# Full-array attention-output products, a four-accumulator first output block and a split last output in a fused attention and feed-forward kernel

## The chip, the cores and the metric

The kernel runs on one core of a Trainium2 chip. The time is the device time of an execution in microseconds; a profile counts from the start of its span, which is about 2 us shorter than the device time. Each kernel ran several times, and runs over 1.5% above the fastest run of the same kernel are left out of comparisons. An eviction is the copy of a result out of PSUM, which frees its buffer. Engines: PE is TensorE (PEld its weight loads), DVE VectorE, ACT ScalarE, POOL GpSimd, SP the engine that issues most transfers.

## The reference

Attention with both softmaxes taken separately (over the head dimension for q, over the sequence for k), so that each head needs only a 64x64 matrix `kv`; then a feed-forward block over all 4,608 tokens. The code is condensed.

```python
batch, n_heads, seq, head_dim = (8, 8, 576, 64)
kv = np.einsum('bhsd,bhse->bhde', k_s, v)          # k_s: softmax over seq
attn = np.einsum('bhsd,bhde->bhse', q_s, kv)       # q_s: softmax over d
x = attn.transpose(0, 2, 1, 3).reshape(B * S, H * D)
h = x @ w_in                                       # 512 -> 2048
g = h + sin(alpha * h) ** 2 / (alpha + 1e-09)
out = g @ w_out                                    # 2048 -> 512
```

## The kernel before

Tokens go in nine tiles of 512. In a tile, "hp" products (h, transposed) go through ACT (sine), one of ACT, POOL or DVE (square) and DVE (combine, which writes g and frees the PSUM buffer of hp). "op" products multiply the g of the previous tile with w_out. The attention of a later batch is woven in: kvp products, kv_norm, then four calls of attn_out per batch, whose result xp is copied to xT, the input of hp. The code below is cut, and its comments are added.

```python
    def attn_out(b, ii, half, pool, eng):
        ...
        xp = pool.tile([128, 2, 512], F32, name="xp", tag="a")
        for x in range(2):
            r = slice(64 * x, 64 * x + 64)
            for e in range(2):
                nc.tensor.matmul(xp[64 * e:64 * e + 64, x, 0:n], kt[r, e, ii, :],
                                 qT[r, j0:j1, ii, e * 64:(e + 1) * 64], start=True, stop=True)
        eng(xT[:, ii::2, c0:c0 + n], xp[:, :, 0:n])
    ...
    opool = ctx.enter_context(tc.tile_pool(name="opool", bufs=3))      # outputs on their way to memory
    ps_h = ctx.enter_context(tc.tile_pool(name="ps_h", bufs=4, space=PSUM, ...))   # hp
    ...
        # tile 0, after its 16 hp: four output blocks, in two pairs (ps_e: two buffers of two banks)
        exp_q(1)
        norm_q(1, [GP, V])
        acc = ps_e.tile([128, 2, dm], F32, name="acc", tag="a")
        os = o_pair(0, 0, [acc[:, 0], acc[:, 1]], [ACT_CP, ACT_CP])
        take(os, 32)
        ...
        os = o_pair(0, 2, [ps_h.tile([128, dm], F32, name="hp", tag="h") for _ in range(2)], [DVE_CP, ACT_CP])
    ...
            # tiles 3 to 8: op products to be done by the end of step ni
            want = 22 + 21 * ni // 8 if b is not None else 4 * (ni + 1)
```

The softmax here doesn't subtract the row's maximum and nothing guards it: scores larger than these inputs give would overflow.

## Time and profile before

| | before |
|---|---|
| device time, median of 4 | 298.85 us (298.34 to 299.05) |
| profiled span | 296.6 us |
| PE busy, share of the span | 94% |
| one 512-column product in a dense stretch | 0.216 us |
| tile with attention, from sixth hp to sixth hp | 30.70 us (142.04 to 172.74) |
| tile 1: its first product (counted back from the second), first product after the tile | 49.9 and 63.7 us |

Read the share of PE first, by slice, then ask of each place where PE stands idle what it waited for. The lines are shown in the prediction below.

### The profile page before, as it was taken

To read this page: it belongs to the slowest core of one execution; us is meant where nothing else is said; L and a number is where in the kernel's file an instruction comes from. 1 tells how busy PE (TensorE), PEld (TensorE's weight loads), DVE (VectorE), ACT (ScalarE), POOL (GpSimd) and SP (SyncE) were. 2 spreads that over 40 slices of the span, in tenths; PEclk is the share of its full clock that TensorE was granted. 3 is DMA by queue.
4 is the path that set the end of the run, shared out by engine and by line. 5 is a ranking of instruction groups with operands and counts; after the bars stand their busy time and mean duration, and the time that the engine had idled before them with its cause. 6 is when DMAs were issued, how large, how long until landed. Compare 5 with 4: busy or idle time off the path is not lost.

```text
span 296.6 us, 4313 instructions
## 1 busy us (share of the span) xinstructions
PE 278.1 (94%) x1595; PEld 127.0 (43%) x1624; DVE 185.5 (63%) x267; ACT 228.5 (77%) x320; POOL 84.6 (29%) x72
## 2 busy tenths in 40 slices
PE   1999998999898999999999999999999999999993
PEld 0444454444343444344444444444444444444441
DVE  2858664889648857764786568656874555555420
ACT  4788666999577899779987998799877777777400
POOL 0949453575755635001600052005000000000000
PEclk9999999999999999999999999999999999999999
DMA  7999979966789966109921894113411111111233
GB/s 263 278 206 200 314 266 298 398 245 184 162 135 368 390 203 128 39 6 331 289 53 23 277 291 98 39 35 69 83 35 35 38 35 35 35 39 43 48 86 71
DMA packets 35540, 45.76 MB, mean 154 GB/s; under 512 B 15792, under 2 KB 20416, under 8 KB 35520
## 3 DMA queue, kind: packets, MB, share of 16 engines
q1 hardware_dynamic: 29520, 34.09, 40.8%
q0 software_dynamic: 5888, 11.27, 15.2%
q8 instruction: 12, 0.20, 0.3%
q10 hardware_dynamic: 112, 0.14, 0.2%
q14 instruction: 8, 0.07, 0.1%
HBM read 36.71 MB, written 9.44 MB: 156 GB/s over the span
## 4 chain that ended last, share of the span: by engine, by line
PE 63%; ACT 15%; DVE 8%; DMA 4%; issue 4%; POOL 3%; SPq 1%; ACTq 0%
PE hp L215 28%; PE op L235 24%; ACT s L221 4%; DVE g L231 4%; ACT ke L111 3%; DMA st_v<-in_v_dram 3%; POOL s L225 2%; PE xp L198 2%; PE acc L235 2%; PE kvp L151 2%; PE hp L235 2%; ACT s L223 2%; ACT L221 2%; ACT L111 2%; ACT qe L111 2%
## 5 line engine op out<-in xcount | busy, mean ns | idle before, releaser
L231 DVE SCALAR_TENSOR_TENSOR g<-s,inva_sb,hp 128x512 bf16<-128x512 f32 x132 | 96.8, 745 | 68.5 <-ACT s L223 54.3
L215 PE MATMUL hp<-xT,win 128*128 128x512 bf16 x515 | 130.5, 379 | 2.7 <-DVE g L231 1.2
L235 PE MATMUL op<-wout,g 128*128 128x512 bf16 x498 | 125.7, 379 | 1.2 <-issue 0.6
L221 ACT ACTIVATE s<-hp,alpha_sb 128x512 f32<-128x512 f32 x132 | 88.9, 681 | 30.4 <-PE hp L215 23.2
L215 PEld LDWEIGHTS <-win 128*128 128x128 bf16 x576 | 55.7, 98 | 70.9 <-issue 4.3
L235 PEld LDWEIGHTS <-g 128*128 128x128 bf16 x576 | 54.1, 98 | 65.4 <-DVE g L231 0.4
L223 ACT ACTIVATE s<-s 128x512 f32<-128x512 f32 x112 | 70.5, 630 | 3.7
L141 POOL TENSOR_TENSOR qn<-qe,qs 128x2304 bf16<-128x2304 bf16 (+1 forms) x8 | 26.6, 3330 | 87.2 <-DVE qs L140 81.7
L225 POOL TENSOR_TENSOR s<-s 128x512 f32<-128x512 f32 x28 | 29.5, 1061 | 23.9 <-ACT s L221 23.8
L139 DVE TENSOR_REDUCE qs<-qe 128x18 f32<-128x1152 bf16 (+1 forms) x11 | 20.7, 1882 | 14.3 <-ACT qe L111 14.2
L241 DVE COPY o<-op 128x512 f32<-128x512 f32 x31 | 21.0, 677 | 10.1 <-PE op L235 10.1
L111 ACT ACTIVATE qe<-st_q 128x1152 bf16<-128x1152 f32 x16 | 17.9, 1155 | 4.8 <-DMA st_q<-in_q_dram 4.7
L111 ACT ACTIVATE ke<-st_k 128x1152 bf16<-128x1152 f32 x16 | 17.7, 1150 | 2.6 <-DMA st_k<-in_k_dram 2.6
L201 DVE CAST xT<-xp 128x512 bf16<-128x512 f32 (+1 forms) x24 | 17.8, 747 | 1.9 <-PE xp L198 1.5
L125 POOL CAST vb<-st_v 128x1152 bf16<-128x1152 f32 x14 | 16.1, 1178 | 8.8 <-DMA st_v<-in_v_dram 8.7
L198 PE MATMUL xp<-qT,kvb 64*64 64x256 bf16 (+1 forms) x128 | 9.7, 302 | 2.7 <-DVE xT L201 1.2
L247 ACT COPY o<-op 64x512 f32<-64x512 f32 x1 | 0.6, 581 | 14.0 <-DVE o L247 14.0
L198 PEld LDWEIGHTS <-kvb 64*64 64x64 bf16 x128 | 4.5, 103 | 13.9 <-issue 11.3
L151 PE MATMUL kvp<-vb,ke 64*128 64x130 bf16 x288 | 9.8, 216 | 0.6 <-DVE qT L181 0.6
L111 ACT ACT_TABLE_LOAD x7 | 9.0, 1283 | 1.3 <-PEq L477 1.2
L151 PEld LDWEIGHTS <-ke 64*128 64x128 bf16 x288 | 8.3, 93 | 3.7 <-issue 2.4
L201 ACT CAST xT<-xp 128x640 bf16<-128x640 f32 (+1 forms) x8 | 5.1, 653 | 5.9 <-PE xp L198 5.9
(52 smaller groups left out, 112.3 us busy)
## 6 DMA issues: line engine op xcount, KB each, us to landing
out_dram<-o SPq DMA_DIRECT2D x71, 128.0 KB, 2.4
st_q<-in_q_dram SPq DMA_DIRECT2D x5, 1152.0 KB, 6.8
st_k<-in_k_dram SPq DMA_DIRECT2D x5, 1152.0 KB, 9.3
st_v<-in_v_dram SPq DMA_DIRECT2D x5, 1152.0 KB, 10.4
st_k<-in_k_dram POOLq DMA_DIRECT2D x2, 1152.0 KB, 12.2
win<-in_moe_w_in_dram POOLq DMA_DIRECT2D x4, 512.0 KB, 8.3
wout<-in_moe_w_out_dram POOLq DMA_DIRECT2D x4, 512.0 KB, 16.3
st_q<-in_q_dram SPq DMA_DIRECT2D x2, 576.0 KB, 4.8
```

What stands on the lines that cost most here:

```text
L111: nc.scalar.activation(dst[:, :, ii * 128:(ii + 1) * 128].rearrange("p j (x d) -> p x j d", x=2), src[:, ii::2], AX.Exp)
L139: nc.vector.tensor_reduce(part, src, axis=AXL.X, op=ALU.add)
L141: engs[h].tensor_tensor(dst, src, part.unsqueeze(3).to_broadcast([128, J, w, D]), op=ALU.mult)
L151: nc.tensor.matmul(kvp[:, e, ii * 130:(ii + 1) * 130], ke[r, j, ii * 128:(ii + 1) * 128], vt[r, j, ii * 130:(ii + 1) * 130], start=(j == 0 ...
L201: eng(xT[:, ii::2, c0:c0 + n], xp[:, :, 0:n])
L215: nc.tensor.matmul(hp, win[:, ki, ni * 128:(ni + 1) * 128], xT[:, ki, t * MF:(t + 1) * MF], start=(ki == 0), stop=(ki == 3))
L221: nc.scalar.activation(s, hp, AX.Sin, scale=alpha_sb[:, ni:ni + 1])
L223: nc.scalar.activation(s, s, AX.Square)
L225: nc.gpsimd.tensor_tensor(s, s, s, op=ALU.mult)
L231: nc.vector.scalar_tensor_tensor(G[t][:, ni], in0=s, scalar=inva_sb[:, ni:ni + 1], in1=hp, op0=ALU.mult, op1=ALU.add)
L235: nc.tensor.matmul(acc, G[t][:, ni, j * 128:(j + 1) * 128], wout[:, ni, :], start=(ni == 0), stop=(ni == nN - 1))
L241: eng(o, acc)
```

## The change

Intent: drop the 64x64 tiling mode of attn_out (two full-array products with a block-diagonal weight instead of four small ones), fetch batch 1 sooner, and shorten the end. Its core, with cuts, shortened lines and added comments:

```diff
+    kbd = [singles.tile([128, 2, 2, 128], BF16, name=f"kbd{n}") for n in range(2)]   # zeroed once
-    win_v = moe_w_in.rearrange("(ko ki) n -> ki ko n", ki=128)
+    win_v = moe_w_in.rearrange("(x c d) n -> x d c n", x=2, c=4)
...
+        for e in range(2):
+            nc.tensor.matmul(xp[:, e, 0:n], kt[:, e, ii], qT[:, j0:j1, ii, e * 64:(e + 1) * 64],
+                             start=True, stop=True)
-        eng(xT[:, ii::2, c0:c0 + n], xp[:, :, 0:n])
+        eng(xT[:, 2 * ii:2 * ii + 2, c0:c0 + n], xp[:, :, 0:n])
...
-        for c in range(4): load_win(c)             # four loads
-        for c in range(4): load_wout(c)
+        for c0, c1 in ((0, 1), (1, 2), (2, 4)): load_win(c0, c1)   # six loads of 64 rows
+        for c in range(3): load_wout(c)            # chunk 3 only after batch 1
...
+    def o_quad(t, accs, engs):                     # all four output blocks of tile 0 at once
+        for c in range(4):
+            for n, m in ([(n, m) for n in range(4) for m in range(4)] if c < 3 else
+                         [(n, m) for m in range(4) for n in range(4)]):
+                mm_o(t, m, 4 * c + n, accs[m])
+                if c == 3 and n == 3:
+                    evac_o(t, m, accs[m], engs[m])
+                yield
...
-        late = {4: ("q", q, 1, True), 7: ("k", k, 1, False), 10: ("v", v, 1, True)}
+        late = {3: ("q", q, 1, True), 6: ("k", k, 1, False), 8: ("v", v, 1, True)}   # ni 11: w_out chunk 3
+        accs = [ps_h.tile([128, dm], F32, name="hp", tag="h") for _ in range(4)]
+        os = o_quad(0, accs, [DVE_CP, ACT_CP, DVE_CP, ACT_CP])
...
-            want = 22 + 21 * ni // 8 if b is not None else 4 * (ni + 1)
+            want = 23 + 21 * ni // 8 if b is not None else 4 * (ni + 1)
...
+    take(o_stream(nT - 1), 48)                     # last output block: two halves of 256 columns,
+    for h in range(2): ...                         # each copied by DVE and stored from SP and ACT
```

Besides, the evictions of batch 3 alternate between ACT and DVE.

## The prediction

> **What bounds the kernel now.** I began with the page's slice table (40 slices of 7.4 us, busy share in tenths) to find which engine is full and where.
>
> ```profile
> PE 278.1 (94%) x1595; PEld 127.0 (43%) x1624; DVE 185.5 (63%) x267; ACT 228.5 (77%) x320; POOL 84.6 (29%) x72
> ...
> PE   1999998999898999999999999999999999999993
> ```
>
> PE (TensorE) is full everywhere but at the two ends; only removed PE work, a removed PE wait, or a shorter head or tail can shorten the run. A matmul record of 379 ns is not its price: in the PE timeline of 143 to 160 us four of them start 0.86 us before the next group, so one 512-column product costs **0.216 us**. The 1,152 products of the two large layers cost 249 us of the 296.6.
>
> The same timeline gives the price of the attention-output group (xp, four 64x64 products).
>
> ```profile
> 150.39 1.03 PE L215 MATMUL hp<-xT,win 128*128 128x512 bf16 x4
> 151.35 0.30 PE L198 MATMUL xp<-qT,kvb 64*64 64x256 bf16 x4
> 151.59 0.82 PE L235 MATMUL op<-wout,g 128*128 128x512 bf16 x3
> 152.24 1.03 PE L215 MATMUL hp<-xT,win 128*128 128x512 bf16 x4
> 153.20 0.33 PE L198 MATMUL xp<-qT,kvb 64*64 64x320 bf16 x4
> 153.46 0.60 PE L235 MATMUL op<-wout,g 128*128 128x512 bf16 x2
> ```
>
> Columns: start, us, engine, line, what. Columns of the hp group run out at 150.39 + 4 x 0.216 = 151.25, yet xp starts at 151.35 and op at 151.59: the group occupies 0.34 us. With 320 columns: 152.24 + 0.864 = 153.10 to 153.46, 0.36 us. The weight-load timeline adds that each first xp weight load comes after 0.42 us of no load, where loads elsewhere run ahead of the products.
>
> Next, the tile boundaries of the steady part (timeline of 172 to 204 us), where PE waits:
>
> ```profile
> 199.96 1.28 ACT L221 ACT_TABLE_LOAD   x1
> ...
> 202.64 0.75 DVE L231 SCALAR_TENSOR_TENSOR g<-s,inva_sb,hp 128x512 bf16<-128x512 f32 x1 [1.19 <-ACT s L223]
> ...
> 203.44 0.81 PE L215 MATMUL hp<-xT,win 128*128 128x512 bf16 x3 [0.16 <-DVE g L231]
> ```
>
> From the end of a tile's first hp, ACT needs a fixed stretch (sine, square, table load, four exps, table load, sine, square), then DVE combines, and only then is a buffer free for the sixth hp. PE fills it with 32 output products and 16 hp products. The op group before ran from 202.47, three products, to 203.12: **0.32 us** of PE time is lost per boundary (0.37 at 111.34).
>
> Then the start, the timeline of 24 to 52 us:
>
> ```profile
> 30.71 1.02 PE L215 MATMUL hp<-xT,win 128*128 128x512 bf16 x4 [0.55 <-DVE g L231]
> 31.57 7.07 PE L235 MATMUL acc<-wout,g 128*128 128x512 bf16 x32
> 31.93 2.07 DVE L231 SCALAR_TENSOR_TENSOR g<-s,inva_sb,hp 128x512 bf16<-128x512 f32 x3
> 33.41 1.04 POOL L225 TENSOR_TENSOR s<-s 128x512 f32<-128x512 f32 x1 [0.86 <-ACT s L221]
> 34.49 0.75 DVE L231 SCALAR_TENSOR_TENSOR g<-s,inva_sb,hp 128x512 bf16<-128x512 f32 x1 [0.49 <-POOL s L225]
> ```
>
> The last hp of tile 0 is done near 31.6, but its combine ends only at 34.49 + 0.75 = 35.24. Today PE does not care: the first output pair writes "acc", other PSUM buffers than hp. And the end:
>
> ```profile
> 287.78 4.05 PE L235 MATMUL op<-wout,g 128*128 128x512 bf16 x17
> 291.86 0.68 DVE L247 COPY o<-op 64x512 f32<-64x512 f32 x1 [2.76 <-PE op L235]
> 292.58 0.58 ACT L247 COPY o<-op 64x512 f32<-64x512 f32 x1 [14.04 <-DVE o L247]
> 293.19 0.55 ACTq L248 DMA_DIRECT2D out_dram<-o  x1
> ```
>
> The two last copies run one after the other; the last store is issued 1.36 us after the last product.
>
> **What the Trainium skill says.** "TensorEngine Tiling (Array Packing)", Key Properties: changing the tiling mode drains TensorE. The trace agrees: the late weight load and the 0.10 us ahead of xp. "TensorE: Matmul & The Clock Gate", Back-to-back issue gap: warm, N/2.4 + 2.5 ns, 216 ns at 512; the trace has 0.216 us. The same page, Part 1, has the array at half clock when cold or after an idle window of about 3.4 us; the trace shows cold warm-up products 0.43 us apart from 6.3 to 9.7 us, and later no gap long enough to test the return. "PSUM — Partial Sum Buffer", Specifications: 8 banks of 512 fp32 per partition; the start uses all eight (four hp buffers of one bank, two of two banks).
>
> **The change part by part.**
>
> 1. Block-diagonal products. Per call, two full-array products of 256 or 320 columns at 0.216/512 per column: 0.216 or 0.270 us, no mode change; the 0.1 us weight loads fit under them. Saved 0.12 and 0.09, so 0.42 us for the four calls of a batch. It counts where PE is the limit: batches 4 to 7, in tiles 3 to 6: 4 x 0.42 = **-1.7 us**. Batches 0 to 3 run where eviction of the single or double xp buffer spaces the calls; there I count it only through parts 3 to 5. Zeroing the two weight tiles falls in DVE's idle start. The evictions move the same data.
>
> 2. One more output product ahead of the boundary (22 becomes 23, 33 instead of 32 before the sixth hp) moves 0.216 us into the 0.32 us wait: four boundaries, **-0.9 us**.
>
> 3. w_in row order. xT pieces 0 and 1 now both come from the first head pair, so hp can do two products, not one, before it needs the second pair's eviction. Worth at most one product: tile 2, whose start waits 0.47 us on ACT's xT, **-0.2**; tile 0 **-0.1**, since the block-diagonal weights are ready 0.3 us later than the first quarter was. Six w_in loads, not four, but the last two carry twice the bytes; last w_in landing today is near 12.5 + 11.7 = 24.2 us, just about when the ninth hp will need it.
>
> 4. Batch 3's evictions alternate ACT and DVE. Today one xp waits 0.86 us for DVE (95.06). The first eviction will stand on ACT behind a square (92.89) and one sine (93.43), so it starts near 94.1, against 94.32 on DVE now; the wait shrinks little: **-0.3 us**.
>
> 5. The start of batch 1. Loading it before the last w_out chunk (1 MB read) should bring q1 some 3 us earlier (today ACT waits 1.45 us for it at 36.09, then 1.85 for k1). But PE does not wait for that now: the transposes at 43.22 follow the products without a gap. What PE meets instead is this: the four accumulators of the new output quad are the **four hp buffers**, and the first four products go to all four. The program's waits confirm that they wait for the combines of hp 12, 13, 14 and 15. So PE, ready near 31.5, does product 4 only at about **35.28**: 3.75 us holding 4 products (0.86), hence 2.9 us lost, in four pieces. After it: 60 products 12.9, 18 transposes 1.0, kv 1.35, four xp calls 1.0, about 0.45 of waits (kv now waits for ACT's copy of the first transposes; second xp pair for an eviction): tile 1 begins near **52.0**. Today its products, counted back from 50.14 less one, begin at 49.92. Net **+2.1 us**; the rest of the old start's waits (0.44, 0.34, 0.25) is what makes it less than 2.9. The last w_out chunk, queued behind v1, should land near 43.5 (v1 lands by 43.4 today, same bytes in all) and is needed at 47.4.
>
> 6. Last output in two halves. A 128x256 copy on DVE should take about 0.4 us (128x512 takes 0.68, with some 0.13 fixed); both stores then go out at once: 0.03 + 0.4 + 0.03 instead of 1.36, **-0.9 us**. Products: 32 of half width cost what 16 of full width do.
>
> Sum: -1.7 - 0.9 - 0.3 - 0.3 + 2.1 - 0.9 = **-2.0 us**, so 298.82 becomes **296.8**.
>
> **The rivals.**
>
> - The start costs nothing. If combines 12 to 15 came earlier, or the wait were hidden by the earlier batch 1, the sum is -4 to -4.5, about 294.5. For it: the loads do come earlier. Against: the combine chain hangs on POOL's squares, and POOL now has six load issues of 0.75 us among them instead of five.
> - The idle stretch cools the array. 3.75 us with 23% of it busy is close to the 3.4 us window; half clock for one window would cost another 1.7 us: 298.5. Against: four products break the gap. I give it 15%.
> - The last w_out chunk or the wider w_in pair lands late: the profile has the DMA engines at 90% or more in slices 2 to 5, 7 and 8. Each us late is a us lost, partly hidden by the wait of part 5: 297 to 299.
> - The 64x64 groups were nearly free, because four run at once in 0.30 us: then part 1 gives little (two serial products 0.22 to 0.27). I trust the start of the next group, which shows 0.34, and not the record. Otherwise 298.
>
> **Range and chances.** Parts 1, 2 and 6 are read off steady patterns, within 0.6 us together. Part 5 is the largest doubt: 0 to +4. Range **295.0 to 298.8**. Faster by over 2% needs less than 292.8, which no mix of terms reaches without extra help in the start: 0.04. Slower by over 2%, 304.8, would need a DMA stall of 8 us: 0.02. Within 2%: 0.94.
>
> **What would show it.** In the changed trace: in the steady tiles xp pairs that occupy 0.22 and 0.27 us with no gap ahead of them; boundary waits at the sixth hp under 0.15 us; PE waiting for DVE g in pieces between 31.5 and 35.3 us, and tile 1's first hp near 52.0; products after that 0.216 us apart (0.43 if cold); the last copy 0.4 us. I am wrong if tile 1 begins before 50.5 or after 53.5, or if the steady tiles do not shorten from 30.70 to about 30.08 us.

## More of the kernel before

One more view of the kernel before: the granted clock (the column after the five engines, 1.00 is full speed) from 32 to 52 us.

```profile
32.00:52.00 20.00, 18.76 (x141) 9.42 (x142) 11.39 (x17) 13.72 (x18) 8.68 (x9) 1.00 0.88 302
```

## The result, and the profile after

The changed kernel took **302.82 us** (302.43 to 303.45, four runs) against 298.85 us. The ratio is 1.0138 (1.0115 to 1.016). A ratio is the mean time of one kernel's fast runs over that of the other's of the same rounds, so it is not quite the ratio of the medians. The time is within 2%, but above the predicted range.

The page of the changed kernel, engine shares and two rows of the slice table:

```profile
PE 279.8 (93%) x1548; PEld 132.8 (44%) x1576; DVE 185.0 (62%) x269; ACT 228.2 (76%) x320; POOL 86.6 (29%) x74
...
PE   2999699799979999999999999999999999999995
...
PEclk9999899999999999999999999999999999999999
```

New in the PE row are the 6 in slice 5 (30 to 38 us) and the 7s in slices 8 and 12. New in the clock row is the 8 in slice 5. The PE timeline of slice 5, output products after the last hp of tile 0:

```profile
32.79 0.38 PE L235 MATMUL hp<-wout,g 128*128 128x512 bf16 x1 [0.95 <-DVE g L231]
33.63 0.38 PE L235 MATMUL hp<-wout,g 128*128 128x512 bf16 x1 [0.47 <-DVE g L231]
34.29 0.38 PE L235 MATMUL hp<-wout,g 128*128 128x512 bf16 x1 [0.28 <-DVE g L231]
35.39 10.50 PE L235 MATMUL hp<-wout,g 128*128 128x512 bf16 x40 [0.73 <-DVE g L231]
```

These are the four pieces of the accumulator wait, the last at 35.39 us where 35.28 was predicted. The weight loads right after it, and the clock of the same 20 us as above:

```profile
36.20 0.15 PEld L235 LDWEIGHTS <-g 128*128 128x128 bf16 x1 [0.28 <-issue]
36.63 0.15 PEld L235 LDWEIGHTS <-g 128*128 128x128 bf16 x1 [0.28 <-issue]
37.05 0.15 PEld L235 LDWEIGHTS <-g 128*128 128x128 bf16 x1 [0.28 <-issue]
```

```profile
32.00:52.00 20.00, 17.30 (x115) 8.38 (x117) 10.85 (x16) 10.83 (x13) 9.56 (x8) 0.91 0.93 313
```

The loads stand 0.43 us apart: the products run at half speed until 38.3 us (from here on a cold array, and at full speed a warm one), and the clock column says 0.91. Then, 20 us later, a wait that the prediction does not have (timeline of 52 to 62 us):

```profile
57.46 0.59 ACT L241 COPY o<-hp 128x512 f32<-128x512 f32 x1 [4.27 <-DMA out_dram<-o]
57.94 1.27 ACT L221 ACTIVATE s<-hp,alpha_sb 128x512 f32<-128x512 f32 x2
58.09 1.02 PE L215 MATMUL hp<-xT,win 128*128 128x512 bf16 x4 [1.54 <-ACT o L241]
```

The fourth output copy of tile 0 needs an output buffer. There are three, and the first comes free only when its store has landed. ACT stands 4.27 us for it, with the sines of tile 1 behind it, and PE cannot start the fourth hp of tile 1, whose buffer that copy empties.

The steady tiles and the end, both from PE, DVE and ACT timelines:

```profile
189.60 0.43 PE L198 MATMUL xp<-qT,kbd 128*128 128x320 bf16 x2
189.87 0.59 PE L235 MATMUL op<-wout,g 128*128 128x512 bf16 x2
190.30 1.03 PE L215 MATMUL hp<-xT,win 128*128 128x512 bf16 x4
...
190.72 0.82 DVE L201 CAST xT<-xp 128x640 bf16<-128x640 f32 x1
...
191.58 0.38 PE L198 MATMUL xp<-qT,kbd 128*128 128x256 bf16 x2 [0.26 <-DVE xT L201]
```

```profile
293.44 3.66 PE L464 MATMUL op<-wout,g 128*128 128x256 bf16 x32
...
297.13 0.42 DVE L241 COPY o<-op 128x256 f32<-128x256 f32 x1 [1.32 <-PE op L464]
```

The pair at 189.60 occupies 0.27 us, as predicted. The third call was ready at 190.30 + 4 x 0.216 = 191.16 and went at 191.58: the eviction of the second had to finish first (190.72 + 0.82 = 191.54).

Where the 4.2 us between the spans lie, by reading the same landmark in both timelines. (The 49.92 is counted back from the second product at 50.14; a lone first product ran at 49.51 and then PE waited, so part of the first two rows' split is a convention.)

| stretch up to | before, us | after, us | added in the stretch |
|---|---|---|---|
| first product of tile 1 | 49.92 | 53.80 | +3.88 |
| kvp of batch 2 (16 hp and 32 op later) | 70.82 | 77.19 | +2.49 |
| first xp of batch 2 | 78.11 | 85.13 | +0.65 |
| sixth hp of tile 3 | 111.34 | 117.93 | -0.43 |
| sixth hp of tile 6 | 203.44 | 209.01 | -1.02 |
| last product done | 291.83 | 297.10 | -0.30 |
| end | 296.6 | 300.8 | -1.07 |

### The profile page after: what moved, and what is told of

Read it like the earlier page. It is cut to its first block, busy times and chain, and to the rows that moved or that the text cites. A ratio compares the mean times of both kernels' runs of the same rounds, so it can differ in the third digit from the quotient of the medians.

```text
span 300.8 us, 4223 instructions
## 1 busy us (share of the span) xinstructions
PE 279.8 (93%) x1548; PEld 132.8 (44%) x1576; DVE 185.0 (62%) x269; ACT 228.2 (76%) x320; POOL 86.6 (29%) x74
## 4 chain that ended last, share of the span: by engine, by line
PE 66%; DVE 12%; DMA 9%; ACT 5%; POOL 4%; issue 3%; SPq 0%; ACTq 0%; POOLq 0%
PE op L235 30%; PE hp L215 26%; DVE g L231 5%; DMA win<-in_moe_w_in_dram 4%; PE hp L235 3%; ACT s L221 3%; POOL s L225 2%; DVE xT L201 2%; PE kvp L154 2%; DMA out_dram<-o 2%; PE xp L198 2%; DMA qT<-qn 2%; DVE o L241 2%; DMA st_q<-in_q_dram 1%; DVE qs L142 1%
## 5 line engine op out<-in xcount | busy, mean ns | idle before, releaser
L235 PE MATMUL op<-wout,g 128*128 128x512 bf16 x480 | 121.1, 379 | 1.4 <-issue 0.5
L241 DVE COPY o<-op 128x512 f32<-128x512 f32 (+1 forms) x33 | 21.9, 663 | 13.3 <-PE op L235 10.9
L128 POOL CAST vb<-st_v 128x1152 bf16<-128x1152 f32 x14 | 17.0, 1245 | 7.3 <-DMA st_v<-in_v_dram 7.3
L235 PE MATMUL hp<-wout,g 128*128 128x512 bf16 x62 | 16.7, 408 | 2.5 <-DVE g L231 2.4
L201 DVE CAST xT<-xp 128x512 bf16<-128x512 f32 (+1 forms) x22 | 16.5, 753 | 2.8 <-PE xp L198 2.7
L198 PE MATMUL xp<-qT,kbd 128*128 128x256 bf16 (+1 forms) x64 | 12.4, 285 | 4.0 <-DMA qT<-qn 1.5
L198 PEld LDWEIGHTS <-kbd 128*128 128x128 bf16 x64 | 6.0, 97 | 12.8 <-issue 5.1
L201 ACT CAST xT<-xp 128x512 bf16<-128x512 f32 (+1 forms) x10 | 6.3, 638 | 7.0 <-PE xp L198 6.9
```

The lines of the kernel that those rows point to most:

```text
L198: nc.tensor.matmul(xp[:, e, 0:n], kt[:, e, ii], qT[:, j0:j1, ii, e * 64:(e + 1) * 64], start=True, stop=True)
L201: eng(xT[:, 2 * ii:2 * ii + 2, c0:c0 + n], xp[:, :, 0:n])
L235: nc.tensor.matmul(acc, G[t][:, ni, j * 128:(j + 1) * 128], wout[:, ni, :], start=(ni == 0), stop=(ni == nN - 1))
L241: eng(o[:, cols], acc)
```

## The experiments

**Theory.** The start pays three things in a row: the accumulator wait, the cold array after it, and the fourth copy's wait for a store. **Rivals** were that these waits just add or hide one another, that the slow products have another cause (weight reads against the transfers), and that a late store only covers another late thing.

### Accumulator order alone

```diff
-            for n, m in ([(n, m) for n in range(4) for m in range(4)] if c < 3 else
-                         [(n, m) for m in range(4) for n in range(4)]):
+            for n, m in [(n, m) for m in range(4) for n in range(4)]:
```

> The changed kernel with one edit: in the output quad of tile 0 each chunk of four weights is finished for one accumulator before the next accumulator starts, so the fourth accumulator is first touched by product 13 instead of product 4. Theory (three waits in a row at the start: the accumulator wait, the cold array after it, and the fourth output copy that waits for a store to land because there are three output buffers): the accumulator wait falls from 2.9 us to about 1.2 us and the array stays warm, so the transposes of batch 1 start near 42.3 us instead of 45.7; but the store wait stays pinned to the landing of the loads of batch 2 near 57 us, so tile 1's fourth hp starts at 57 to 58 as before and the whole run gains only 0 to 1.5 us (301.3 to 302.8). Rival (the start's waits simply add up, nothing pins them): 3.4 us gained, 299.4.

Measured: 303.56 us, ratio to before 1.0147 (1.0115 to 1.0179): nothing gained, and 0.8 us above the expected range. The PE timeline, start of tile 1:

```profile
50.85 2.75 PE L215 MATMUL hp<-xT,win 128*128 128x512 bf16 x12
57.62 1.87 PE L215 MATMUL hp<-xT,win 128*128 128x512 bf16 x4 [4.02 <-ACT o L241]
```

Tile 1 begins 2.95 us earlier (50.85 for 53.80), and its fourth hp is still at 57.6. Most of the saved time (2.48 of 2.95 us) reappears as a longer wait for the same store (4.02 for 1.54 us), and that idle stretch cools the array: the four products after it take 1.87 us instead of 1.02. One run of the four stayed warm (clock 1.000, 301.76 us), the others had 0.988 and 303.37 to 303.88 us.

### Four output buffers alone

```diff
-    opool = ctx.enter_context(tc.tile_pool(name="opool", bufs=3))
+    opool = ctx.enter_context(tc.tile_pool(name="opool", bufs=4))
```

> The changed kernel with one edit: four output buffers instead of three. Theory: the fourth copy of tile 0 no longer waits for a store, tile 1's fourth hp starts near 56.4 instead of 58.1 and the two later combine waits of tile 1 (0.43 and 0.41 us) go too: 2.5 us gained, about 300.3. Rival (the late store only covers another late thing, such as the loads of batch 2): under 1 us gained, over 301.8. The accumulator wait and the cold products stay (first products at 32.8, 33.6, 34.3, 35.4; the next eight 0.43 us apart).

Measured: 300.70 us in the median; fast runs 299.15, 300.34 and 301.06, one slow run (304.25, clock 0.983, no trace kept) left out; ratio 1.0046 (1.0014 to 1.0078). Two fast runs have a clock of 0.993; they average 300.70, which is 2.2 us under the changed kernel's mean of 302.88. So the store wait cost 2.2 us, near the 2.5 us expected. The run at 299.15 us has a clock of 0.999, and it is the profiled one: the same four pieces of waiting (33.13, 33.97, 34.63, 35.74), then products at full speed. The same program after the same waits runs cold in some executions and warm in others. In the two profiles, the stretch from product 4 to the transposes is 45.73 - 35.39 = 10.34 us cold and 44.59 - 35.74 = 8.85 us warm: the cold array costs 1.5 us.

### Both

Both diffs above.

> The changed kernel with both edits (accumulator order, four output buffers). Theory: 2.5 us of the store wait plus 1.7 us of the accumulator wait plus 1.7 us of the cold array: about 297.0, and a granted clock of 1.0. Rival (another limit takes over at the start, such as the query chain that ends near 41.1 us or the last w_out chunk): 298.5 or more.

Measured: 297.61 us, ratio 0.9965 (0.9939 to 0.999): 5.2 us under the changed kernel and a little faster than the kernel before. All four runs have a clock of 0.999 or 1.000. The PE timeline:

```profile
33.37 9.67 PE L235 MATMUL hp<-wout,g 128*128 128x512 bf16 x43 [0.95 <-DVE g L231]
...
50.95 3.62 PE L215 MATMUL hp<-xT,win 128*128 128x512 bf16 x16
```

One piece of waiting is left, and tile 1 runs through. Alone the edits gave 0 and 2.2 us, together 5.2 us. The rival of waits that simply add is refuted: the order pays only once the store no longer pins tile 1.

### Dummy products in the gaps, with four output buffers

```diff
+                if c == 0 and n == 0:
+                    for _ in range((5, 2, 2, 3)[m]):
+                        nc.tensor.matmul(junk, identb, A["qe", 0][:, 0:4, 0:128], start=True, stop=True)
                 mm_o(t, m, 4 * c + n, accs[m])
```

> The changed kernel with four output buffers and 12 dummy products in the gaps of the accumulator wait (their results are not used), so the wait stays and only the idle array goes. Theory: the products after the fourth are 0.216 us apart instead of 0.43, which is 8 times 0.21 or 1.7 us less than the run with four output buffers alone: about 298.6. Rival (the slow products are not an effect of the idle time, but of something else in that stretch, such as the weight reads against the DMA traffic): no difference from the run with four output buffers alone.

Measured: 299.27 us (298.92 to 300.1), ratio 1.002 (1.0 to 1.0039), clock 0.997 to 1.000 in all four runs. The wait itself stays:

```profile
34.07 0.38 PE L235 MATMUL hp<-wout,g 128*128 128x512 bf16 x1
...
36.67 9.01 PE L235 MATMUL hp<-wout,g 128*128 128x512 bf16 x40
```

From the first output product to the fourth it is 2.60 us, as in the changed kernel (32.79 to 35.39), but the 40 products after it take 9.01 us instead of 10.50. Work that computes nothing removed the slow products, so idleness made them slow. The time equals that of the warm run with four output buffers alone (299.15), and is 1.4 us under its cold ones (300.70). It is 0.7 us above the number expected; this profile waits 1.0 us for w_in, which is looked at below.

### The last output in halves alone, on the kernel before

The tail of the change, nothing else.

> The kernel before with one part of the change alone: the last output in two halves. Theory: the last store is issued 0.46 us after the last product instead of 1.36, so 0.9 us are gained (the changed kernel ended 3.70 us after its last product, the one before 4.77): 298.0. Rival (the end is set by the landing of all stores of the last tile, whatever their order): no gain.

Measured over five rounds: 298.03 us, ratio 0.9979 (0.9966 to 0.9991), which is 0.6 us (0.3 to 1.0). The gain is real and somewhat smaller than the 0.9 us counted. Its copy takes 0.42 us, as in the changed kernel. In the changed kernel's profile the stretch from last product to end fell by 1.07 us, here by 0.42. Why it is less here is not found.

### The block-diagonal products alone, on the kernel before

Full-array products, kbd, row order of w_in in six loads; start, evictions and the count of 22 as before.

> The kernel before with the block-diagonal products and the matching w_in rows alone (six w_in loads as in the changed kernel; start order, evictions and the count of 22 as before). Theory from the traces: the products of a batch cost 0.98 us of PE instead of 1.40, but the third call of a batch then waits for the second eviction on DVE, because one buffer serves all four calls, so a tile with attention shortens by 0.1 to 0.2 us and not by 0.42: 0.4 to 0.8 us in all, less 0.3 to 1.0 us of waiting for the wider last w_in pair: 298.2 to 299.2. Rival (the prediction's count): 1.7 us gained in the steady tiles, 297.2.

Measured: 299.27 us, ratio 1.0023 (1.0008 to 1.0039): 0.7 us slower than before, just above the expected range, and far from the 297.2 us of the prediction's count. Two sixth-hp lines of steady tiles:

```profile
142.70 1.02 PE L214 MATMUL hp<-xT,win 128*128 128x512 bf16 x4 [0.16 <-DVE g L230]
173.28 1.02 PE L214 MATMUL hp<-xT,win 128*128 128x512 bf16 x4 [0.16 <-DVE g L230]
```

The tile takes 30.58 us, only 0.12 less than before. In the changed kernel it takes 30.36 (178.65 to 209.01), so the one output product moved ahead (23 for 22) is worth the 0.22 us that the prediction gave it. Why the tile shortens so little can be read in the kernel before, DVE and PE of a steady tile:

```profile
184.81 0.81 DVE L201 CAST xT<-xp 128x640 bf16<-128x640 f32 x1
...
185.67 0.30 PE L198 MATMUL xp<-qT,kvb 64*64 64x256 bf16 x4
```

The eviction of the second call ends at 185.62, and the third call follows at once. So the single xp buffer held the third call in the kernel before too. From the first call to the third it is 3.62 us there (182.05 to 185.67) and 3.72 us here (151.91 to 155.63), so up to the third call the cheaper products save nothing.

The new waits of this run: 0.6 us for w_in, and 1.5 us instead of 0.8 for the transposing DMA of batch 2. Why that DMA lands later in this program is not found. It does so in most of these kernels, but not with late loads of batch 2 and not in the last run below (0.8 us in both).

### w_in in four chunks of two halves, on "both"

```diff
-        for c0, c1 in ((0, 1), (1, 2), (2, 4)):
+        for c0, c1 in ((0, 1), (1, 2), (2, 3), (3, 4)):
```

> The run with accumulator order and four output buffers, and besides w_in loaded as four chunks of two halves instead of three groups. Theory: the wait of the ninth hp for w_in (0.5 us there, 0.3 to 1.0 in the runs so far) goes, because its 512 columns no longer land together with the next 512: 0.3 to 0.5 us gained, 297.1. Rival (the weights are late because the transfers as a whole are late): the wait stays, 297.6.

Measured: 297.03 us, ratio 0.9947 (0.993 to 0.9965); "both" had 0.9965. The wait for w_in is gone from the profile and about 0.5 us of time with it, as the theory said, though the two intervals overlap.

### Second and fourth eviction on ACT, on "both": a miss

```diff
-                attn_back(b, ni - 5)
+                attn_back(b, ni - 5, (ACT_CP, DVE_CP))
```

> The run with accumulator order and four output buffers, and besides in the steady tiles the second and fourth eviction of a batch on ACT instead of DVE. Theory (DVE's row of combine, eviction, output copy, eviction makes the third call wait 0.42 us of PE time in each of four tiles): the wait goes, 1.0 to 1.6 us gained, 296.0 to 296.6. Rival (ACT's sines come late because of the evictions and the hp buffers with them): no gain or a loss.

Measured: 297.38 us, ratio 0.9964 (0.9944 to 0.9984): no gain. The third and the fourth call in a steady tile:

```profile
155.32 0.38 PE L198 MATMUL xp<-qT,kbd 128*128 128x256 bf16 x2
...
157.60 0.43 PE L198 MATMUL xp<-qT,kbd 128*128 128x320 bf16 x2 [0.39 <-DVE xT L201]
```

The third call no longer waits, but the fourth does (0.39 us), since on DVE the eviction of the third stands behind a combine that waits 1.25 us for ACT's square, and ACT is later by the eviction it took over. The wait moved by one call. With one PSUM buffer for four calls, the evictions hold a call in either order. Whether a second buffer would set the gain free is not tested; the buffers of hp, op and xp fill all eight banks.

### Loads of batch 2 after the stores of tile 0, three output buffers

```diff
-        for name, x in (("q", q), ("k", k), ("v", v)):
-            load(name, x, 2, eng=GP)
...
         take(os)
+        load_batch(2)
```

> The changed kernel, still with three output buffers, but the loads of batch 2 issued after the stores of tile 0 instead of ahead of them. Theory (the fourth copy waits because its store lands late behind the 3.5 MB of batch 2): the stores land 2 to 3 us after their issue, the wait of the fourth hp of tile 1 is gone or under 0.3 us, and the run takes what it took with four output buffers: 299.2 (array warm) to 301.0 (array cold). Rival (a store takes 5 us at this place anyway): the wait stays and the time is 302.8.

Measured: 300.64 us; 298.92 at clock 1.000, and 300.52 to 301.43 at 0.994; ratio 1.0055 (1.0025 to 1.0085). The tile view of the eight stores of tile 0, first in the changed kernel, then here:

```profile
DMA to landing us min/median/max: 2.2/4.0/5.9
```

```profile
DMA to landing us min/median/max: 2.3/2.3/2.5
```

The stores land in 2.3 us once the 3.5 MB of batch 2 are not ahead of them, and PE's wait disappears with three buffers. So those loads made the store late. It was not the order within one queue: in the changed kernel POOL issues the loads (from 43.19 us) and SP the stores (from 51.19 us), and from 46 to 56 us the DMA engines move 356 to 412 GB/s. The edit also moves the loads from POOL to SP, which no run tests alone.

### The old load order, on "both"

All four w_out chunks ahead of batch 1, batch 1 at the old places.

> The run with accumulator order and four output buffers (297.61), but with all four w_out chunks ahead of batch 1 and batch 1 issued at the old places. Theory (loading batch 1 earlier buys nothing because PE, not the query chain, sets the start): the normalized queries are ready at 42.5 us against a PE that reaches the transposes at 42.9, so no difference beyond 0.4 us: 297.2 to 298.0. Rival (the earlier loads are what the order of the quad needs): 1.5 us or more lost, over 299.0.

Measured: 297.74 us, ratio 0.9966 (0.9947 to 0.9985): the same as "both". The transposes wait 0.34 us for the queries, no more. Loading batch 1 ahead of the last w_out chunk bought nothing in this program.

### The start of tile 0 undone: the fastest version

The changed kernel with o_pair and the old load order, w_in in four chunks of two halves; the other parts kept.

> The changed kernel with the start of tile 0 undone (output pairs with accumulators outside the hp buffers, old load order) and w_in in four chunks; block-diagonal products, count of 23, alternating evictions of batch 3 and the last output in halves stay. Theory: no accumulator wait, no cold array, no store wait, so what is left are the gains: 0.34 us in each of four tiles, 0.3 to 0.5 in tile 2, 0.6 to 1.0 at the end, less the longer wait for the transposing DMA (0.6): 296.2 to 297.0, faster than the kernel before by 0.6 to 0.9%. Rival (the gains in the changed kernel lean on its new start): 298 or more.

Measured over five rounds: 296.92 us (296.73 to 297.15), ratio 0.9938 (0.9921 to 0.9955), by the ratio 1.9 us under the kernel before. It beats both kernels. The rival is refuted: the gains do not lean on the new start.

## Why the prediction was wrong

- **The step that failed is part 5, the sum of the start.** The accumulator wait itself was right to the detail: the four accumulators waited for the combines of hp 12 to 15, and product 4 went at 35.39 us (35.28 predicted). But "tile 1 begins near 52.0" took that as the whole cost, +2.1 us. The start cost 3.88 us up to tile 1, which began at 53.80, and 2.49 more within it.
- The first missing term was a named rival, "the idle stretch cools the array", put at 15% and 1.7 us. It came in all four runs of the changed kernel (clock 0.992 to 0.994) and cost 1.5 us. The argument against it, that four products break the gap, was wrong: they fill 0.86 of 3.75 us, and that was too little. The dummy products show the cause. That it comes in some executions and not in others is not explained.
- The second missing term was a wait nobody looked for: four output copies within some 3 us on three output buffers (the first three start at 50.47, 51.81 and 53.14), with stores behind the loads of batch 2. It cost about 2 us, shown in two ways (2.2 us with a fourth buffer; 2.0 with later loads, cold runs against cold runs). In the kernel before these stores took up to 7.2 us to land, but it copied two blocks at 42.7 and two at 49.8, so three buffers were enough.
- As an estimate, these two (3.7 us), w_in (0.28 us in the profile), the later transposing DMA (0.65) and the next point (1.2) make 5.8 of the 6.0 us between 296.8 and 302.8.
- **Part 1 was over-counted.** The PE cost of a pair was right (0.27 us), the sum was not: -1.7 us was counted, and 0.12 us in each of four tiles, -0.5, came. The evictions of the single xp buffer took the rest back. The prediction had seen this limit for batches 0 to 3 and taken PE as the limit in the steady tiles; but in the steady tiles of the kernel before the third call already went only when the eviction of the second had ended (185.62 and 185.67 us). With part 2 the tile went from 30.70 to 30.36 us, not to the 30.08 predicted.
- Part 2 was right (0.22 us per boundary). In part 6 the copy was right (0.42 for 0.4 us), and the gain alone is 0.6 us of the 0.9. The stretch with tile 2 shortened by 0.43 us, near the 0.5 that parts 3 and 4 counted there; no run separates the two. The w_in loads came late by 0.3 to 1.0 us, as one of the rivals feared; four chunks remove it.
- The judgement on the earlier loads was right: PE did not wait for batch 1.

## What to carry to other kernels

When accumulators are moved to buffers of another stage, list what each buffer must be emptied of and what it empties into: here both ends, the combines before and the output stores after, held TensorE. Ask of every new TensorE wait what it does to the clock, because here a sprinkling of products did not keep the array warm in most executions. And when two waits lie in a row behind a pinned event, removing the first alone shows nothing; remove both before judging either.

## What the Trainium skill lacked or had wrong

- "TensorE: Matmul & The Clock Gate", Why this matters for your kernels, tells one to allow no idle gap over about 3 us between bursts of products. That is not enough. Here no single wait before a product was over 0.95 us, yet 3.75 us with 0.86 us of products in them were followed by products 0.43 us apart. The run with both edits had one wait of the same 0.95 us and stayed at a clock of 0.999 or 1.000 in all four executions, so the longest wait did not decide. The page's section on a second HAM failure mode does say that frequent short idles can do it, but gives no size. The page's remark on run-to-run variation speaks of the start of a kernel; here, in the middle of three programs (accumulator order alone, four output buffers alone, late loads), one execution of four stayed warm (judged by the clock, which was 0.999 or 1.000 against 0.988 to 0.994 in the other fast ones, 1.6 to 2.0 us apart).
- "TensorEngine Tiling (Array Packing)", Key Properties, says that a change of mode drains the engine and gives no size. Here a 64x64 group of 256 columns between full-array products occupied 0.34 us, of which 0.10 passed before its first product; two full-array products took 0.22 us, so the packing of four gained nothing.
- No page gives what a small store costs behind large loads: a 128 KB store landed 2.3 us after its issue with no such load ahead of it, and up to 5.9 us after it behind 3.5 MB (8.9 in the run with the accumulator order alone).
- "TensorE: Matmul & The Clock Gate", Back-to-back issue gap, calls the 216 ns that the prediction took from it the gap of an isolated product, and gives about 131 ns for a sustained stream at 512 columns. Here a sustained stream ran at 216 ns a product.
